# Two transformer layers on one core: one engine per PSUM tile, ScalarE takes the first plain copy of a slot, and the FFN norm is applied a slot later

## The chip, the cores and the metric

The kernel runs on one core of one Trainium2 chip. The metric is device time in microseconds; lower is better. TensorE (PE) does the matmuls, VectorE (DVE), ScalarE (ACT) and GpSimd (POOL) the element-wise work, and SyncE (SP) issues the DMAs. Each engine works through its own queue in order.

## The reference

Two blocks, run twice over x of 2048 rows and 512 columns in bfloat16. The attention block has 32 heads of 16 columns and a sliding window of 256 rows; the feed-forward block (FFN) is 512 to 1792 to 512 with ReLU.

```python
def _A_ref(x, wqkv, wo):
    ...
    scores = jnp.einsum("bhqd,bhkd->bhqk", q, k) * (Dh ** -0.5)
    ...
    mask = (idx[:, None] - idx[None, :] >= 0) & (idx[:, None] - idx[None, :] < W)
    scores = jnp.where(mask[None, None], scores, -1e9)
    p = _softmax(scores, axis=-1)
    o = jnp.einsum("bhqk,bhkd->bhqd", p, v)
    return (lambda x, *d: x.transpose(*d))(o, 0, 2, 1, 3).reshape(B, S, D) @ wo
...
x = x + _A_ref(_layernorm(x, axis=-1), A_wqkv, A_wo)
x = x + _B_ref(_layernorm(x, axis=-1), B_w1, B_w2)
x = x + _A_ref(_layernorm(x, axis=-1), A_wqkv, A_wo)
x = x + _B_ref(_layernorm(x, axis=-1), B_w1, B_w2)
```

## The kernel before

**Chunks and slots.** The rows are cut into four chunks of 512, so two layers make eight chunks, numbered 0 to 7 here. The program is a list of 160 slots (`NS`), 20 for each chunk (`SPS`). Slot s of chunk k does one group of attention scores for one of four head sets t and one of five groups of key blocks g: TensorE writes scores to the PSUM tile `Sps` (one buffer of four banks), ScalarE takes the exponential of it into `Pb`, and one slot later the group's triangular masks are laid on `Pb`, by GpSimd for g = 1 and 2 and by VectorE for the others. Five slots later, in slots with g of 1 to 4, TensorE multiplies `Pb` with V (24 matmuls into a tile `acc`), and VectorE divides by the sum into `O` (`pv_group`). So a slot with g = 0, which is slot 0, 5, 10 and 15 of a chunk, has no such product.

**The rest of the work fills the slots.** Projections to Q, K and V of the next chunk, the output projection `wo`, and the FFN (`w1`, then `w2`) are tasks cut into single matmuls. `run_tasks` takes tasks by earliest due slot, some nine matmuls a slot, two thirds of them ahead of the product with V and the rest behind it. A task can't start before its `early` slot. Each task accumulates in a PSUM tile `ps_d`, of which there are four, shared with `acc`, and is then copied out:

- Q (`q_items`): one copy of 128x512 to `Qt`, by ScalarE.
- K (`k_items`): two copies of the same tile to `KBD`, each with every second head set to zero by the factor `par`: the first by VectorE, the second by ScalarE (in chunks 1 and 6 each is split in two, since the ring of 20 key blocks wraps).
- V (`v_items`): four copies of 64x256 to `V2f`, by VectorE and ScalarE in turn.
- `w1` (`w1_item`): ReLU to `hT`, by VectorE. `wo` and `w2`: an addition to `x_sb`, by VectorE.

**From attention to the FFN.** In slots 1 to 4 of a chunk the last product with V of the chunk before comes out for rows j = 0 to 3; SyncE then transposes that `O` by DMA to `OT`, and `wo` for j may run two slots later. When `wo` for j = 1 and j = 3 is issued, `wo_done` calls `ln_rows`: VectorE takes the statistics of two row blocks, GpSimd finishes them (`rstdB`, `nbB`) and writes the normalised rows `xnB`, and SyncE transposes these to `xn2T`. All at once: `ln_rows` issues both the statistics and the application. With j = 3 the FFN tasks are planned, with their `early` slot three further on:

```python
def wo_done(k, j):
    ...
    if j % 2:
        ln_rows(c, xn2T[k], "B", j - 1, j + 1)
    if j == 3:
        plan_ffn(k, now[0] + 3)
```

**What sets the order.** `InOrder` chains TensorE, VectorE, ScalarE and GpSimd in the order of the code. SyncE is not chained: the framework's scheduler puts its DMAs in the order in which it expects them to become ready. The framework also puts a wait between two engines that read the same PSUM tile, so that they take it in turn.

Of the kernel before, what the change touches and what calls it, by code (L numbers as in the profile page):

```python
# [13 lines left out]
ACT = mybir.ActivationFunctionType  # L14
ALU = mybir.AluOpType
# [34 lines left out]
def kernel(  # L50
# [31 lines left out]
    chained = [True]  # L82
# [19 lines left out]
    pe, dve, act, pool = InOrder(nc.tensor), InOrder(nc.vector), InOrder(nc.scalar), InOrder(nc.gpsimd)  # L102
# [96 lines left out]
    def ln_rows(c, xnT, sfx, j0, j1):  # L199
        ln_apply(c, xnT, sfx, j0, j1, ln_stats(c, sfx, j0, j1))  # L200
# [2 lines left out]
    def slot(layer, kb):  # L203
        return (32 * layer + kb) % NSLOT

    def q_items(xnT, Qt, t, direct=False):
        ps = []

        def one(kc):
            if kc == 0:  # L210
                ps.append(ps_d.tile([P, 512], FP32, name="ps_d"))
            mm(ps[0][:], wqkv[:, kc, t * P:(t + 1) * P], xnT[:, kc, :], kc == 0, kc == KC - 1)
            if kc == KC - 1:
                (act.copy if chained[0] and not direct else dve.tensor_copy)(Qt[:], ps[0][:])
        return [lambda kc=kc: one(kc) for kc in range(KC)]

    def k_items(layer, c, xnT, t):
        ps = []
        s0 = slot(layer, 8 * c)
        runs = [(0, 8)] if s0 + 8 <= NSLOT else [(0, NSLOT - s0), (NSLOT - s0, 8)]  # L220

        def one(kc):
            if kc == 0:
                ps.append(ps_d.tile([P, 512], FP32, name="ps_d"))
            mm(ps[0][:], wqkv[:, kc, D + t * P:D + (t + 1) * P], xnT[:, kc, :], kc == 0, kc == KC - 1)
            if kc < KC - 1:
                return
            for a, b in runs:
                sa = (s0 + a) % NSLOT
                for e in range(2):  # L230
                    o = KBD[:, t, sa:sa + b - a, e, :]
                    i = ps[0][:, 64 * a:64 * b].rearrange("p (s k) -> p s k", k=64)
                    if e:
                        act.activation(o, i, ACT.Copy, scale=par[:, 1:2])
                    else:
                        dve.tensor_scalar(out=o, in0=i, scalar1=par[:, 0:1], scalar2=None, op0=ALU.mult)
        return [lambda kc=kc: one(kc) for kc in range(KC)]

    def v_items(layer, c, xnT, j):
        ps = []  # L240

        def one(kc):
            if kc == 0:
                ps.append(ps_d.tile([P, 512], FP32, name="ps_d"))
            mm(ps[0][:], xnT[:, kc, j * P:(j + 1) * P], wqkv[:, kc, 2 * D:3 * D], kc == 0, kc == KC - 1)
            if kc < KC - 1:
                return
            v4 = ps[0][:].rearrange("p (a e d) -> p e a d", e=2, d=16)
            for half in range(2):
                sl = slot(layer, 8 * c + 2 * j + half)  # L250
                for e in range(2):
                    (act.copy if e else dve.tensor_copy)(V2[64 * e:64 * e + 64, sl, e, :, 0:16],
                                                         v4[64 * half:64 * half + 64, e])
        return [lambda kc=kc: one(kc) for kc in range(KC)]


# [93 lines left out]
    def w1_item(xnT, hT, f):  # L350
        ps = []

        def one(kc):
            if kc == 0:
                ps.append(ps_d.tile([P, 512], FP32, name="ps_d"))
            mm(ps[0][:], w1[:, kc, f * P:(f + 1) * P], xnT[:, kc, :], kc == 0, kc == KC - 1)
            if kc == KC - 1:
                dve.tensor_relu(hT[:, f, :], ps[0][:])
        return [lambda kc=kc: one(kc) for kc in range(KC)]

    def w2_items(c, hT, j, final):
# [20 lines left out]
    NS = NSTEP * SPS  # L382
# [3 lines left out]
    def at_slot(s, fn):  # L386
        events.setdefault(s, []).append(fn)
# [53 lines left out]
    def plan_qkv(k, base):  # L441

        layer, c = divmod(k, NCH)

        def q_make(t):
            Q[k, t] = work.tile([P, 512], BF16, name="Qt", bufs=7)
            return q_items(xnTs[k], Q[k, t], t, k == 0)
        order = [("K0", 1), ("Q0", 2), ("K1", 3), ("Q1", 4), ("K2", 5), ("Q2", 6), ("K3", 7), ("V0", 8), ("V1", 9), ("V2", 10),
                 ("V3", 11), ("Q3", 12)]
        if k == 0:  # L450
            order = [("K0", 0), ("Q0", 0), ("V0", 1), ("V1", 1), ("V2", 1), ("V3", 1), ("K1", 2), ("Q1", 2), ("K2", 5),
                     ("Q2", 5), ("K3", 8), ("Q3", 8)]
        for what, due in order:
            n = int(what[1])
            if what[0] == "K":
                Task(base, base + due, base + SPS + 5 * n - 3, KC, lambda n=n: k_items(layer, c, xnTs[k], n))
            elif what[0] == "Q":
                Task(base + (6 if n == 3 else 1) if k else 0, base + due, base + SPS + 5 * n - 1, KC, lambda n=n: q_make(n))
            else:
                Task(base + 7 if k else 0, base + due, base + SPS + 3, KC, lambda n=n: v_items(layer, c, xnTs[k], n))  # L460
# [22 lines left out]
    def wo_done(k, j):  # L483
        layer, c = divmod(k, NCH)
        if j == 0:
            xn2T[k] = work.tile([P, KC, 512], BF16, name="xn2T", bufs=1)
        if j % 2:
            ln_rows(c, xn2T[k], "B", j - 1, j + 1)
        if j == 3:
            plan_ffn(k, now[0] + 3)  # L490

    now = [0]
    planned = [0]
# [30 lines left out]
    for s in range(NS + 5):  # L524
        now[0] = s
        u, g = divmod(s, 5)
        k, t = divmod(u, 4)
        layer, c = divmod(k, NCH)
        rest = sum(y.n for y in tasks) + 128 * (NSTEP - 1) - planned[0]
        budget = -(-rest // (NS - s)) if s < NS else 0  # L530
        has_pv = u >= 1 and g >= 1
        if s < NS:
            force(s)
            masks.append(attn_group(layer, c, t, g, Q[k, t], u % 2))
        for fn in events.pop(s, []):
            fn()
        done = run_tasks(s, -(-(budget + (3 if has_pv else 0)) // 2))
        if len(masks) > (1 if s < NS else 0):
            masks.pop(0)()
        if has_pv:  # L540
            pk, ptt = divmod(u - 1, 4)
            j = g - 1
            if ptt == 0 and j == 0:
                O_of[pk] = work.tile([P, 4, D], BF16, name="O", tag="O", bufs=1)
                chk_of[pk] = work.tile([P, 4, 32], FP32, name="chk")
            pv_group(pk // NCH, pk % NCH, ptt, j, (u - 1) % 2, O_of[pk], chk_of[pk])
            if ptt == 3:
                OTs[pk, j] = transpose_o(O_of[pk][:, j, :])
                plan_wo(pk, j, s + 2)
                if j == 3:  # L550
                    accumulate_check(chk_of[pk], badacc, first=(pk == 0))
        run_tasks(s, budget - done)
# [129 lines left out]
```

## Time and profile before

| What | us |
|---|---|
| median of two runs (619.52 and 620.05) | 619.78 |
| profiled execution | 618.08 |
| its span, first to last instruction | 616.4 |
| mean granted TensorE clock (share of full speed) | 0.905 |

The rows quoted below come from the profiled execution. Its own time is 1.7 us over its span, and 1.7 us under the median of the two other runs.

### The profile page before, as it was taken

What the parts mean: (1) busy time and instruction counts of PE and PEld (TensorE: products, weight loads), DVE (VectorE), ACT (ScalarE), POOL (GpSimd) and SP (SyncE); (2) the same over time, 40 slices, a digit from 0 to 9 for tenths busy, and PEclk for the clock granted to TensorE, in tenths of its full rate; (3) what the DMA queues carried; (4) which work ended last, traced back from release to release, by engine and by line L of the source; (5) the groups of instructions that cost most, each with busy time, mean ns of one, the idle gap of its engine ahead of it and who ended that gap; (6) DMA issues with size and microseconds to landing.
All of it is one profiled execution on the core that took longest, in us unless ns stands there. A gap on an engine that the chain in (4) does not pass through costs nothing.

```text
span 616.4 us, 13901 instructions
## 1 busy us (share of the span) xinstructions
PE 492.1 (80%) x5741; PEld 237.4 (39%) x5741; DVE 348.9 (57%) x919; ACT 345.9 (56%) x299; POOL 255.0 (41%) x558
## 2 busy tenths in 40 slices
PE   6748467689968998699958996799777996898395
PEld 2314233345423453344523442444433543344142
DVE  6444545477456847476456745685465637554461
ACT  2447668466757667566645565657737767462000
POOL 6562354437314544428224642446325444431300
PEclk9879659799978999899979998999988999898799
DMA  8610011201011011201110111002220013002201
GB/s 278 234 35 1 1 36 27 44 2 37 18 35 19 6 32 37 35 2 37 27 27 18 28 27 36 18 2 55 33 35 18 3 36 55 16 10 54 43 1 40
DMA packets 59001, 23.02 MB, mean 37 GB/s; under 512 B 50480, under 2 KB 58416, under 8 KB 58928
## 3 DMA queue, kind: packets, MB, share of 16 engines
q1 hardware_dynamic: 58928, 22.03, 15.6%
q8 instruction: 47, 0.77, 0.6%
q14 instruction: 26, 0.21, 0.1%
HBM read 7.86 MB, written 2.10 MB: 16 GB/s over the span
## 4 chain that ended last, share of the span: by engine, by line
PE 53%; ACT 16%; DVE 14%; DMA 5%; POOL 5%; issue 3%; SPq 2%; POOLq 0%; ACTq 0%; DVEq 0%
PE ps_d L94 40%; ACT Pb L94 12%; PE acc L94 7%; PE Sps L94 6%; DMA OT<-O 4%; DVE V2f L94 3%; ACT V2f L94 3%; DVE stB L94 2%; SPq L196 2%; POOL xnB L94 2%; DVE x_sb L94 2%; DVE KBD L94 2%; POOL rstdB L94 1%; DVE O L94 1%; DMA xnT<-xnA 1%
## 5 line engine op out<-in xcount | busy, mean ns | idle before, releaser
L94 ACT ACTIVATE Pb<-Sps 128x2048 bf16<-128x2048 f32 (+2 forms) x160 | 283.2, 1770 | 106.0 <-PE Sps L94 100.5
L94 POOL TENSOR_SCALAR_AFFINE_SELECT Pb<-Pb 64x256 bf16<-64x256 bf16 x368 | 154.2, 419 | 171.5 <-ACT Pb L94 146.5
L94 PE MATMUL ps_d<-xn2T,w 128*128 128x512 bf16 x448 | 118.9, 400 | 14.7 <-DMA xn2T<-xnB 13.2
L94 PE MATMUL ps_d<-w,hT 128*128 128x512 bf16 x448 | 110.8, 381 | 0.0
L94 PEld LDWEIGHTS <-Pb 128*128 128x128 bf16 x2880 | 92.6, 97 | 34.9 <-issue 9.1
L94 PE MATMUL Sps<-Qt,KBD 32*128 32x320 bf16 (+4 forms) x1408 | 64.6, 266 | 48.2 <-ACT Pb L94 46.8
L94 DVE TENSOR_SCALAR hT<-ps_d 128x512 bf16<-128x512 f32 x112 | 76.6, 687 | 38.5 <-PE ps_d L94 37.3
L94 PE MATMUL acc<-V2f,Pb 128*128 128x34 bf16 x2880 | 94.5, 180 | 0.9 <-DVE chk L94 0.8
L94 PE MATMUL ps_d<-xnT,wqkv 128*128 128x512 bf16 x256 | 78.1, 423 | 8.3 <-DMA xnT<-xnA 6.7
L94 PE MATMUL ps_d<-wo,OT 128*128 128x512 bf16 x128 | 40.3, 443 | 39.1 <-DMA OT<-O 39.1
L94 PEld LDWEIGHTS <-KBD 32*128 32x128 bf16 x1408 | 26.8, 93 | 115.2 <-issue 112.6
L94 PEld LDWEIGHTS <-w 128*128 128x128 bf16 x448 | 38.7, 100 | 61.7 <-issue 30.8
L94 DVE TENSOR_TENSOR x_sb<-ps_d,x_sb 128x512 f32<-128x512 f32 x48 | 32.9, 688 | 51.5 <-PE ps_d L94 50.9
L94 DVE TENSOR_TENSOR Pb<-Pb,tri 128x512 bf16<-128x512 bf16 (+1 forms) x152 | 59.9, 428 | 0.8 <-ACT Pb L94 0.8
L94 DVE RECIPROCAL chk<-acc 128x8 f32<-128x8 f32 x128 | 26.1, 204 | 59.4 <-PE acc L94 58.0
L94 POOL TENSOR_TENSOR rstdB<-rstdB,mhalf 128x2 f32<-128x2 f32 x16 | 12.0, 753 | 106.9 <-DVE rstdB L94 106.9
L94 PEld LDWEIGHTS <-hT 128*128 128x128 bf16 x448 | 37.9, 97 | 42.9 <-issue 6.6
L94 DVE CAST V2f<-ps_d 64x256 bf16<-64x256 f32 x64 | 27.0, 421 | 35.7 <-ACT V2f L94 32.9
L94 ACT ACTIVATE KBD<-ps_d,par 128x512 bf16<-128x512 f32 (+1 forms) x40 | 24.1, 604 | 38.2 <-DVE KBD L94 37.9
L94 DVE TENSOR_SCALAR KBD<-ps_d,par 128x512 bf16<-128x512 f32 (+1 forms) x40 | 25.5, 639 | 31.6 <-PE ps_d L94 21.1
L94 DVE TENSOR_TENSOR O<-acc,chk 128x128 bf16<-128x128 f32 x128 | 37.3, 291 | 8.9 <-DMA OT<-O 4.5
L94 ACT CAST V2f<-ps_d 64x256 bf16<-64x256 f32 x64 | 23.5, 368 | 31.2 <-DVE V2f L94 30.7
(65 smaller groups left out, 297.5 us busy)
## 6 DMA issues: line engine op xcount, KB each, us to landing
w<-in_B_w_dram SPq DMA_DIRECT2D x2, 1792.0 KB, 13.6
out_dram<-ob SPq DMA_DIRECT2D x16, 128.0 KB, 1.7
wqkv<-in_A_wqkv_dram SPq DMA_DIRECT2D x3, 512.0 KB, 6.7
xst<-in_A_x_dram SPq DMA_DIRECT2D x3, 512.0 KB, 8.7
xst<-in_A_x_dram SPq DMA_DIRECT2D x2, 256.0 KB, 2.9
wo<-in_A_wo_dram SPq DMA_DIRECT2D x1, 512.0 KB, 8.7
OT<-O SPq DMA_TRANSPOSE x32, 2.4
xn2T<-xnB SPq DMA_TRANSPOSE x32, 2.4
```

What stands on the lines that cost most here:

```text
L94: inst = fn(*a, **k)
L196: nc.sync.dma_start_transpose(out=xnT[:, :, j * P:(j + 1) * P], in_=xn[:].rearrange("p (kc d) -> p kc d", kc=KC))
```

## The change

There are three edits.

1. A new helper `evacuate` copies a PSUM tile out with one engine. In each slot after the first, the first plain copy (Q) or ReLU (`w1`) that the first call of `run_tasks` issues goes to ScalarE; all others go to VectorE.
2. The two copies of K and the four copies of V are all VectorE's.
3. `wo_done` takes the statistics as before but puts the application (`xnB` and its transposes) into a later slot: two slots on for j = 1 and one slot on for j = 3. The FFN may start four slots on, not three. After the last slot nothing is put off.

```diff
--- before.py
+++ after.py
@@ -203,7 +203,19 @@
     def slot(layer, kb):
         return (32 * layer + kb) % NSLOT
 
-    def q_items(xnT, Qt, t, direct=False):
+    act_turn = [False]
+
+    def evacuate(o, i, relu=False):
+
+        if act_turn[0]:
+            act_turn[0] = False
+            act.activation(o, i, ACT.Relu if relu else ACT.Copy)
+        elif relu:
+            dve.tensor_relu(o, i)
+        else:
+            dve.tensor_copy(o, i)
+
+    def q_items(xnT, Qt, t):
         ps = []
 
         def one(kc):
@@ -211,7 +223,7 @@
                 ps.append(ps_d.tile([P, 512], FP32, name="ps_d"))
             mm(ps[0][:], wqkv[:, kc, t * P:(t + 1) * P], xnT[:, kc, :], kc == 0, kc == KC - 1)
             if kc == KC - 1:
-                (act.copy if chained[0] and not direct else dve.tensor_copy)(Qt[:], ps[0][:])
+                evacuate(Qt[:], ps[0][:])
         return [lambda kc=kc: one(kc) for kc in range(KC)]
 
     def k_items(layer, c, xnT, t):
@@ -230,10 +242,7 @@
                 for e in range(2):
                     o = KBD[:, t, sa:sa + b - a, e, :]
                     i = ps[0][:, 64 * a:64 * b].rearrange("p (s k) -> p s k", k=64)
-                    if e:
-                        act.activation(o, i, ACT.Copy, scale=par[:, 1:2])
-                    else:
-                        dve.tensor_scalar(out=o, in0=i, scalar1=par[:, 0:1], scalar2=None, op0=ALU.mult)
+                    dve.tensor_scalar(out=o, in0=i, scalar1=par[:, e:e + 1], scalar2=None, op0=ALU.mult)
         return [lambda kc=kc: one(kc) for kc in range(KC)]
 
     def v_items(layer, c, xnT, j):
@@ -249,8 +258,7 @@
             for half in range(2):
                 sl = slot(layer, 8 * c + 2 * j + half)
                 for e in range(2):
-                    (act.copy if e else dve.tensor_copy)(V2[64 * e:64 * e + 64, sl, e, :, 0:16],
-                                                         v4[64 * half:64 * half + 64, e])
+                    dve.tensor_copy(V2[64 * e:64 * e + 64, sl, e, :, 0:16], v4[64 * half:64 * half + 64, e])
         return [lambda kc=kc: one(kc) for kc in range(KC)]
 
 
@@ -355,7 +363,7 @@
                 ps.append(ps_d.tile([P, 512], FP32, name="ps_d"))
             mm(ps[0][:], w1[:, kc, f * P:(f + 1) * P], xnT[:, kc, :], kc == 0, kc == KC - 1)
             if kc == KC - 1:
-                dve.tensor_relu(hT[:, f, :], ps[0][:])
+                evacuate(hT[:, f, :], ps[0][:], relu=True)
         return [lambda kc=kc: one(kc) for kc in range(KC)]
 
     def w2_items(c, hT, j, final):
@@ -444,7 +452,7 @@
 
         def q_make(t):
             Q[k, t] = work.tile([P, 512], BF16, name="Qt", bufs=7)
-            return q_items(xnTs[k], Q[k, t], t, k == 0)
+            return q_items(xnTs[k], Q[k, t], t)
         order = [("K0", 1), ("Q0", 2), ("K1", 3), ("Q1", 4), ("K2", 5), ("Q2", 6), ("K3", 7), ("V0", 8), ("V1", 9), ("V2", 10),
                  ("V3", 11), ("Q3", 12)]
         if k == 0:
@@ -485,9 +493,13 @@
         if j == 0:
             xn2T[k] = work.tile([P, KC, 512], BF16, name="xn2T", bufs=1)
         if j % 2:
-            ln_rows(c, xn2T[k], "B", j - 1, j + 1)
+            st = ln_stats(c, "B", j - 1, j + 1)
+            if now[0] >= NS:
+                ln_apply(c, xn2T[k], "B", j - 1, j + 1, st)
+            else:
+                at_slot(now[0] + (2 if j == 1 else 1), lambda: ln_apply(c, xn2T[k], "B", j - 1, j + 1, st))
         if j == 3:
-            plan_ffn(k, now[0] + 3)
+            plan_ffn(k, now[0] + 4 if now[0] < NS else now[0])
 
     now = [0]
     planned = [0]
@@ -534,7 +546,9 @@
             masks.append(attn_group(layer, c, t, g, Q[k, t], u % 2))
         for fn in events.pop(s, []):
             fn()
+        act_turn[0] = 0 < s < NS
         done = run_tasks(s, -(-(budget + (3 if has_pv else 0)) // 2))
+        act_turn[0] = False
         if len(masks) > (1 if s < NS else 0):
             masks.pop(0)()
         if has_pv:
```

Since the FFN tasks become ready one slot later, `run_tasks` fills the slots in another order from chunk 1 on. Counted from the order of TensorE's instructions: slot 9 of chunk 1 loses its nine FFN matmuls, slot 10 of chunk 2 and slot 9 of chunk 7 run none, and slots 10 of chunks 4 and 6 run one each. The FFN of each chunk therefore ends later, and in chunks 2 to 6 its last `w2` matmuls stand ahead of the third or fourth `wo` group.

**TensorE, chunk 2, the start of the products of slot 6** (`Sps` are scores, `OT` with `wo` is the output projection of j = 3, `hT` with `w_87`, which is `w2`, is the FFN). Before:

```order
L94 MATMUL Sps<-Qt,KBD 128x192
L94 LDWEIGHTS KBD
L94 MATMUL Sps<-Qt,KBD 128x192
L94 LDWEIGHTS OT
L94 MATMUL ps_d<-wo,OT 128x512
```

Now:

```order
L94 MATMUL Sps<-Qt,KBD 128x192
L94 LDWEIGHTS KBD
L94 MATMUL Sps<-Qt,KBD 128x192
L94 LDWEIGHTS hT
L94 MATMUL ps_d<-w_87,hT 128x512
```

The `wo` groups of j = 2 and 3 have moved behind 13 FFN matmuls (nine in slot 5 and four here); the one of j = 3 now ends in slot 7.

**SyncE, chunk 3 and the transposes of x for the next one** (`OT<-O` are the four attention outputs, `xn2T<-xnB` the normalised rows for the FFN, `xnT<-xnA` those for Q, K and V). Before:

```order
L332 DMA_TRANSPOSE OT<-O 128x4x128 x3
L196 DMA_TRANSPOSE xn2T<-xnB 128x4x128 x2
L332 DMA_TRANSPOSE OT<-O 128x4x128
L196 DMA_TRANSPOSE xn2T<-xnB 128x4x128 x2
L196 DMA_TRANSPOSE xnT<-xnA 128x4x128 x4
```

Now, with the start of chunk 4 behind it:

```order
L340 DMA_TRANSPOSE OT<-O 128x4x128 x4
L196 DMA_TRANSPOSE xn2T<-xnB 128x4x128 x4
L196 DMA_TRANSPOSE xnT<-xnA 128x4x128 x4
L340 DMA_TRANSPOSE OT<-O 128x4x128 x3
L196 DMA_TRANSPOSE xn2T<-xnB 128x4x128
```

In chunks 3 and 5 the last `O` is no longer behind two transposes of `xnB`; in chunks 1, 2, 4 and 6 one of the two is still ahead of it. In chunk 7 none was ahead before either.

**VectorE, chunk 3, from the product with V of slot 6** (a RECIPROCAL and the O behind it close one product; `V2f` are copies of V, `stB` to `rstdB` the statistics). Before:

```order
L94 RECIPROCAL chk<-acc 128x8
L94 TENSOR_TENSOR O<-acc,chk 128x128
L94 CAST V2f<-ps_d 64x16x16 x2
L94 RECIPROCAL chk<-acc 128x8
L94 TENSOR_TENSOR O<-acc,chk 128x128
L94 CAST V2f<-ps_d 64x16x16 x4
L94 RECIPROCAL chk<-acc 128x8
L94 TENSOR_TENSOR O<-acc,chk 128x128
L94 CAST V2f<-ps_d 64x16x16 x2
L94 TENSOR_SCALAR hT<-ps_d 128x512
```

Now, from the second statistics of that chunk on:

```order
L94 TENSOR_SCALAR rstdB<-mvB 128x2
L94 RECIPROCAL chk<-acc 128x8
L94 TENSOR_TENSOR O<-acc,chk 128x128
L94 TENSOR_TENSOR x_sb<-ps_d,x_sb 128x512
L94 RECIPROCAL chk<-acc 128x8
L94 TENSOR_TENSOR O<-acc,chk 128x128
L94 CAST V2f<-ps_d 64x16x16 x12
L94 TENSOR_TENSOR Pb_133<-Pb_133,tri 128x4x2x64
L94 TENSOR_TENSOR Pb_133<-Pb_133,tri 128x4x128
L94 RECIPROCAL chk<-acc 128x8
L94 TENSOR_TENSOR O<-acc,chk 128x128
L94 CAST V2f<-ps_d 64x16x16 x4
```

VectorE makes 16 copies of V in a chunk where it made eight, twelve of them in a row, behind the statistics. Over the kernel ScalarE loses 64 copies of V, 40 of K and six of Q and gains 45 ReLU; VectorE the reverse.

## Rows read from the trace of the kernel before

**Rows 1.** Part 1 of the page: busy time, share and instructions by engine.

```profile
PE 492.1 (80%) x5741; PEld 237.4 (39%) x5741; DVE 348.9 (57%) x919; ACT 345.9 (56%) x299; POOL 255.0 (41%) x558
```

**Rows 2.** Windows: chunk 3, its slots 5, 6, 8, 10, 11, and 5 to 11.

```profile
core 0: us, PE busy (x) PEld busy (x) DVE busy (x) ACT busy (x) POOL busy (x), PEclk, DMA share, GB/s
227.05:294.99 67.94, 58.31 (x749) 29.01 (x748) 42.57 (x112) 44.72 (x37) 31.07 (x68) 0.97 0.14 25
...
241.72:247.25 5.53, 2.23 (x16) 0.82 (x16) 4.74 (x16) 2.47 (x4) 2.67 (x5) 1.00 0.13 27
247.25:254.14 6.89, 4.37 (x42) 1.97 (x43) 2.34 (x7) 2.35 (x4) 0.00 (x0) 0.75 0.18 36
259.05:263.96 4.91, 2.94 (x45) 1.65 (x45) 2.10 (x7) 3.35 (x5) 3.30 (x9) 1.00 0.29 27
266.39:268.85 2.46, 2.46 (x18) 0.97 (x17) 1.77 (x4) 1.88 (x1) 0.00 (x0) 1.00 0.00 0
268.85:271.85 3.00, 3.00 (x42) 1.52 (x41) 2.31 (x6) 1.88 (x2) 1.00 (x2) 1.00 0.03 5
241.72:271.85 30.13, 20.81 (x244) 10.01 (x245) 18.50 (x52) 17.15 (x19) 11.32 (x24) 0.94 0.14 23
```

**Rows 3.** Timeline, chunk 3: start, us, engine, operation, [idle before <-releaser].

```profile
243.08 0.29 DVE L94 TENSOR_TENSOR O<-acc,chk 128x128 bf16<-128x128 f32 x1
...
246.66 0.69 ACT L94 ACTIVATE KBD<-ps_d,par 128x512 bf16<-128x512 f32 x1 [3.06 <-DVE KBD L94]
...
247.31 1.19 SPq L332 DMA_TRANSPOSE OT<-O  x1
...
249.77 0.61 PE L94 MATMUL ps_d<-wo,OT 128*128 128x512 bf16 x1 [5.34 <-DMA OT<-O]
```

**Rows 4.** Chain that ended last, chunk 3: start us, us, what.

```profile
239.76 0.69 DVE x_sb L94
...
243.84 1.53 POOL xnB L94 x2
...
245.92 1.22 SPq L196
...
247.31 2.41 DMA OT<-O
...
258.20 0.44 DVE V2f L94
...
258.66 0.38 ACT V2f L94
...
259.05 1.88 ACT Pb L94
...
266.29 1.83 PE ps_d L94 x8
```

**Rows 5.** Waits, whole kernel: who waited for whom, us in total, times, longest.

```profile
PE Sps L94 <- ACT Pb L94: 46.8, 42, 3.3
...
PE ps_d L94 <- DMA OT<-O: 39.1, 14, 6.3
...
PE ps_d L94 <- DMA xn2T<-xnB: 13.2, 2, 9.4
```

**Rows 6.** Groups of instructions by form, whole kernel: xcount | busy us, mean ns | idle before.

```profile
L94 POOL TENSOR_SCALAR_AFFINE_SELECT Pb<-Pb 64x256 bf16<-64x256 bf16 x368 | 154.2, 419 | 171.5 <-ACT Pb L94 146.5 <-PE acc L94 7.8
...
L94 DVE TENSOR_SCALAR hT<-ps_d 128x512 bf16<-128x512 f32 x112 | 76.6, 687 | 38.5 <-PE ps_d L94 37.3
...
L94 DVE CAST V2f<-ps_d 64x256 bf16<-64x256 f32 x64 | 27.0, 421 | 35.7 <-ACT V2f L94 32.9 <-PE ps_d L94 2.2
...
L94 ACT CAST V2f<-ps_d 64x256 bf16<-64x256 f32 x64 | 23.5, 368 | 31.2 <-DVE V2f L94 30.7
...
L94 DVE BATCH_NORM_STATS2 stB<-x_sb 128x6 f32<-128x512 f32 x32 | 21.5, 672 | 0.0
...
L94 DVE TENSOR_SCALAR KBD<-ps_d,par 128x512 bf16<-128x512 f32 x24 | 17.9, 744 | 14.3 <-PE ps_d L94 14.3
...
L94 ACT CAST Qt<-ps_d 128x512 bf16<-128x512 f32 x28 | 16.3, 588 | 27.7 <-PE ps_d L94 27.1
```

## The prediction

> **What bounds the kernel now.** I read the busy shares first: TensorE 80%, VectorE 57%, ScalarE 56% [rows 1]. Nothing is full, so the question is in which slots TensorE stands still. I therefore cut one regular chunk into its slots, from one exponential to the next [rows 2]. An undisturbed slot takes 2.46 us without a product with V (slot 10) and 3.00 us with one (slot 11); TensorE is busy all through both. Sixteen and four of these would make 57.8 us a chunk; chunk 3 takes 67.94. The ten microseconds lie in slots 5 to 8: 5.53 and 6.89, then twice 4.91 (slot 7 is as long as slot 8). Two mechanisms make them.
>
> *The wait for the last attention output.* TensorE stands 5.34 us ahead of the `wo` group of j = 3 [rows 3]. `O` is ready at 243.4, but its transpose is issued at 247.31: SyncE has two transposes of `xnB` ahead of it, and these wait on statistics, then GpSimd. The chain of waits runs through exactly this [rows 4]: x_sb at 239.76, `xnB` at 243.84, the second transpose at 245.92, `OT` at 247.31, landing 2.41 later. Over the kernel TensorE waits 39.1 us so [rows 5]; six long ones, one in each of chunks 1 to 6, make most of it. In that slot the clock falls to 0.75, and the four matmuls behind the wait pay for it.
>
> *The V copies.* VectorE and ScalarE take the same tile in turn, 0.44 and 0.38 us, with no overlap: 258.20, 258.66, then the exponential at 259.05 [rows 4]. The exponential of the next slot stands in ScalarE's queue behind four such hand-overs, and scores have one buffer, so TensorE waits for the exponential: 46.8 us over the kernel [rows 5].
>
> **The change part by part.** The sum is made against the span of 616.4 us; the median lies 3.4 us over it.
>
> *Slots 5 to 11 of a chunk, where the three edits meet.* They take 30.13 us with VectorE busy 18.50 [rows 2]. TensorE alone would need two slots of 2.46 and five of 3.00, 19.9 us: the floor if nothing waits. VectorE's own work in the new order, between the product of slot 4 and that of slot 11, is the other bound. To the 18.5 come eight V copies at 0.421, one K copy at 0.744, one Q copy and two additions (0.69 each, as the ReLU of the same shape), and a pair of statistics that has moved in (twice 0.672 and some 0.5 for the small steps); five ReLU copies of 0.687 go to ScalarE or later slots [rows 6]. That is 18.5 + 3.4 + 0.7 + 2.1 + 1.8 - 3.4 = 23.1 us. So the stretch ends between 19.9 + some stalls and 23.1. Lateness of VectorE can run on into slots 12 to 15, where the ReLU copies have become fewer, but twelve V copies in a row (5.1 us) must hold up the four tiles for a while. I take 22.7, a gain of 7.4, near VectorE's bound, since that is the row with the least freedom.
>
> That needs the wait for `OT` to be gone. In chunk 3 the transpose goes first in SyncE's new order: `O` at 243.4, issued at once, landing 2.4 later; TensorE reaches the group only after some 15 matmuls at 0.23 (eight take 1.83 [rows 4]) and two sets of scores, above 4 us. Covered. In chunks 2, 4 and 6 one transpose of `xnB` is still ahead. From the x_sb addition (239.76) to the first transpose's end is 6.1 us (245.9), and 2.5 more to landing: 8.6. TensorE has between 7 and 8.5 us of work before the group, thanks to the 13 or 14 `w2` matmuls. So waits of about 1.4, 0.6 and 0 remain, +2 in all. Five chunks (2 to 6): -37.
>
> *Chunk 1.* TensorE's order is the old one up to slot 8, so its wait stays and shortens by one transpose of 1.22 [rows 4]. The V slots gain: 9.8 + 2.4 + 2.5 before for slots 7 to 10, against some 12 of VectorE work. -4.
>
> *Chunks 0 and 7.* In chunk 0 the second K copy delays the first scores by 0.744, and two V slots can lose what slot 8 shows over slot 11, 1.9 each: between +0.7 and -3, taken -1. In chunk 7 TensorE waits 3.8 us for `xn2T` (13.2 less the 9.4 of the end [rows 5]); the FFN starts a slot later, so one product with V runs in that wait: between 0 and -2.5, taken -1. The tail behind the last slot is unchanged: there VectorE copies as before and the norm is not put off.
>
> *K copies in slots 1 to 4.* ScalarE's waits for VectorE delay an exponential there too, but TensorE has other matmuls: costed at nothing, the cover being its projections. VectorE's second copy, 0.744, lies in slots where it is idle a third of the time.
>
> *The ReLU and Q copies on ScalarE.* 1.88 for the exponential and 0.588 for a copy make 2.47 [rows 2, 6], within a slot of 3.00 and just that of 2.46. Waiting behind it is the next exponential; the copy's matmuls stand ahead of that exponential's scores on TensorE anyway. Nothing.
>
> *Slots without FFN work.* The later start leaves slots in which TensorE has no task. I price each slot at the larger of 2.46 and 0.53 + 0.213 a matmul + 0.52 for a product with V (this fits slots 10 and 11), over the counts of both orders, with the shorter exponentials of chunks 0 and 4: 432.8 us before, 438.7 now. +6.
>
> *The later norm.* In chunks 2 and 6 six mask steps of 0.419 (2.5 us) come ahead of `xnB` for j = 2, 3 on GpSimd. From the addition to landing the chain needs 9.9 us (239.76 to 247.2, and 2.4 [rows 4]); with the masks 12.4, against four slots, 11.4. A new wait of 1 us in two chunks: +2.
>
> Sum: -37 + 2 - 4 - 1 - 1 + 6 + 2 = -33 us. 619.8 - 33 = **587 us**.
>
> One rule speaks against the move of V to VectorE. The rows have a V copy at 0.421 us there and at 0.368 on ScalarE: 64 copies cost 3.4 us more, which is in the sum. The Trainium skill, Perfetto Trace Analysis, Optimizing Scalar/DVE Operations, gives VectorE the larger overhead on PSUM (~125 ns against ~51 ns) and would take work off VectorE where it is saturated. By its figures the 64 copies would cost an estimated 4.7 us more, so the sum would move by 1 us; its second half is the first rival.
>
> **The rivals.**
>
> 1. *VectorE is the bound and never catches up.* For: 23.1 of 30 us, then statistics of the next norm soon after. Against: from slot 11 on it is busy 2.31 of 3.00 [rows 2] and loses ReLU copies. Half the gain in five chunks is lost: -33 + 18 = -15, 605 us. Chance 0.2.
> 2. *Slower than before: the FFN waits for `xn2T` in each of seven chunks.* Such waits are there already, 3.8 and 9.4 us. If the fourth `wo` addition comes late, behind V copies (5.1 us), the chain of 9.9 to 12.4 becomes 15 to 17.5 against 11.4 us. It decides when VectorE is more than about 1.5 us behind at that addition. Some 5 us and 1 us of lower clock in seven chunks: +42, 629 us. Against: the order has the statistics ahead of the V copies. Chance 0.05.
> 3. *The edits meet no bound.* The wait for `OT` only turns into one for tiles, as the V copies still take 16 times 0.421 in series: 610 to 620 us. Against: the exponentials leave that series, 1.88 us each. Chance 0.07.
> 4. *All cover holds.* Slots 5 to 11 at 21 us: five times 1.7 more, no new waits: 574 us. Chance 0.1.
>
> **How the numbers follow.** The forecast, 576 to 600, has 0.58. The range reaches from rival 4 to rival 1 and a little beyond, 571 to 609. A measurement of this kernel tells about 2% from no change, that is below 607.4 or above 632. Faster by that: 0.58, 0.1, most of rival 1 and a little of rival 3, together 0.84. Same 0.12. Slower 0.04.
>
> **What would show it.** In the profile after: slots 5 and 6 at some 3 us with no wait for `OT` above 2 us in chunks 2 to 6, and one of about 4 in chunk 1; no ScalarE time in V or K; ScalarE's busy time down by some 25 us (V 23.5, K about 25 as on VectorE, six Q copies 3.5, against 45 ReLU at about 0.588 [rows 6]) and VectorE's up by as much; V slots at 3 to 4 us with VectorE full; slots without tasks at 2.46. The forecast is wrong if TensorE's wait for `xn2T` grows beyond some 6 us in all ahead of the tail, or if VectorE is full from slot 4 to slot 15.

## The result, and the profile after

The changed kernel takes 570.09 us (median of two runs, 569.97 and 570.20) against 619.78: a ratio of 0.9198, 95% interval 0.9159 to 0.9238. The forecast of 587 us had the direction and the two main mechanisms. But the gain is 49.7 us where it had 33, and the time lies 1 us under the low end of its range (571 to 609): on the size the prediction was wrong. The profiled execution has a span of 568.3 us (616.4 before).

Part 1 of the page, to be read against [rows 1]. VectorE's busy time has risen by 23.0 us and ScalarE's has fallen by 23.8; TensorE's share has risen to 83%.

```profile
PE 473.9 (83%) x5649; PEld 233.2 (41%) x5741; DVE 371.9 (65%) x984; ACT 322.1 (57%) x234; POOL 255.9 (45%) x558
```

Windows of chunk 3: the chunk, its slots 5, 6, 8, 10 and 11, and 5 to 11, as in [rows 2].

```profile
core 0: us, PE busy (x) PEld busy (x) DVE busy (x) ACT busy (x) POOL busy (x), PEclk, DMA share, GB/s
208.82:269.08 60.26, 56.81 (x741) 28.33 (x752) 45.94 (x119) 42.04 (x29) 31.77 (x68) 1.00 0.14 28
223.15:225.61 2.46, 2.33 (x17) 0.92 (x17) 2.36 (x9) 1.88 (x1) 0.00 (x0) 1.00 0.33 57
225.61:229.36 3.75, 3.36 (x41) 1.43 (x41) 3.68 (x9) 1.88 (x1) 2.55 (x5) 1.00 0.00 0
...
232.31:235.30 2.99, 2.88 (x45) 1.55 (x45) 2.39 (x10) 1.88 (x2) 2.11 (x5) 1.00 0.03 5
238.23:241.53 3.30, 2.59 (x17) 0.84 (x17) 3.16 (x8) 2.48 (x3) 2.90 (x7) 1.00 0.01 2
241.53:246.00 4.47, 3.45 (x41) 1.53 (x42) 4.33 (x12) 2.36 (x2) 2.32 (x5) 1.00 0.00 0
223.15:246.00 22.85, 20.38 (x244) 9.40 (x247) 21.60 (x58) 14.22 (x9) 12.84 (x27) 1.00 0.16 30
```

Slots 5 and 6 have come down from 5.53 and 6.89 us to 2.46 and 3.75, slot 8 from 4.91 to 2.99. The granted clock of slot 6 is 1.00, where it was 0.75. The stretch takes 22.85 us with VectorE busy 21.60. What it has over the 19.9 us of TensorE's own slots lies in slots 6, 10 and 11: TensorE waits there 0.29 and 1.09 us for VectorE (slots 6 and 11) and 0.57 us for the FFN's rows (slot 10). VectorE is the fullest engine of the stretch, but that it alone sets its length is not shown.

The timeline at the place of [rows 3]: `O`, its transpose, and the `wo` group that reads it.

```profile
222.84 0.29 DVE L94 TENSOR_TENSOR O<-acc,chk 128x128 bf16<-128x128 f32 x1
...
223.22 1.77 SPq L340 DMA_TRANSPOSE OT<-O  x1
...
226.14 0.82 PE L94 MATMUL ps_d<-wo,OT 128*128 128x512 bf16 x3
```

The transpose is issued 0.09 us after `O` is ready, where it was 3.9, and TensorE starts the group 2.9 us after the issue, with no idle time ahead of these matmuls.

The chain that ended last, in the same chunk, in place of [rows 4]:

```profile
230.34 0.60 DVE x_sb L94
230.94 0.61 DVE stB L94
...
232.92 0.72 POOL rstdB L94
...
234.31 1.53 POOL xnB L94 x2
235.84 0.46 SPq L196
236.39 2.43 DMA xn2T<-xnB
...
239.07 1.99 PE ps_d L94 x8
```

It no longer goes through `OT`, nor through copies in turn by two engines, but from the last addition of `wo` over the norm to `xn2T`: the FFN starts 0.25 us after its rows have landed, behind the 0.57 us of waiting for them. So the FFN, a slot later, has nothing to spare.

TensorE's waits over the kernel, against [rows 5]:

```profile
PE Sps L94 <- ACT Pb L94: 19.8, 20, 2.0
...
PE ps_d L94 <- DMA OT<-O: 14.7, 10, 4.9
PE ps_d L94 <- DMA xnT<-xnA: 11.9, 2, 11.0
PE ps_d L94 <- DMA xn2T<-xnB: 11.0, 3, 9.6
```

The two waits of the forecast have fallen from 46.8 and 39.1 to 19.8 and 14.7 us. Groups by form, against [rows 6]:

```profile
L94 DVE CAST V2f<-ps_d 64x256 bf16<-64x256 f32 x128 | 54.2, 423 | 3.3 <-PE ps_d L94 1.5
...
L94 DVE TENSOR_SCALAR KBD<-ps_d,par 128x512 bf16<-128x512 f32 x48 | 33.5, 743 | 14.9 <-PE ps_d L94 13.3 <-PE Sps L94 1.6
```

A copy of V or K costs VectorE what it did (0.421 and 0.744 us before); its idle time ahead of the V copies has gone from 35.7 us, 32.9 of it spent on ScalarE, to 3.3.

Where the time came from, from the starts of the exponentials in the two profiled executions (chunk k, slot s to slot t):

| Stretch | before | after | difference | forecast |
|---|---|---|---|---|
| chunk 0 | 64.84 | 58.87 | -6.0 | -1 |
| chunks 1 to 6, slots 0 to 4 (six summed) | 95.16 | 87.80 | -7.4 | 0 |
| chunk 1, slots 5 to 11 | 30.26 | 25.68 | -4.6 | -4 |
| chunks 2 to 6, slots 5 to 11 (five summed) | 150.89 | 118.59 | -32.3 | -33 |
| chunk 7, slots 5 to 11 | 24.52 | 22.13 | -2.4 | -1 |
| chunks 1 to 7, slots 12 on, and the tail | 214.91 | 219.41 | +4.5 | +6 |

The forecast of -33 for the five chunks is its -37 with the two terms of +2, for `OT` and for the later norm. Two rows vary between executions of the same code: chunk 0 takes 58.68 to 60.05 us in the eight profiled kernels that have the changed one's chunk 0, and the tail, from the start of the last exponential, 56.73 to 58.50 us over all 18 profiled kernels.

### The profile page after: what moved, and what is told of

Its sections match the earlier page's. It is cut to its first block, busy times and chain, and to the rows that moved or that the text cites. A ratio compares the mean times of both kernels' runs of the same rounds, so it can differ in the third digit from the quotient of the medians.

```text
span 568.3 us, 13813 instructions
## 1 busy us (share of the span) xinstructions
PE 473.9 (83%) x5649; PEld 233.2 (41%) x5741; DVE 371.9 (65%) x984; ACT 322.1 (57%) x234; POOL 255.9 (45%) x558
## 4 chain that ended last, share of the span: by engine, by line
PE 62%; DVE 19%; DMA 6%; POOL 5%; issue 4%; ACT 2%; SPq 0%; DVEq 0%; POOLq 0%; ACTq 0%
PE ps_d L94 46%; PE acc L94 9%; PE Sps L94 7%; DVE V2f L94 4%; DMA OT<-O 4%; DVE stB L94 3%; DVE x_sb L94 2%; DVE KBD L94 2%; DVE Pb L94 2%; ACT Pb L94 2%; DMA xn2T<-xnB 1%; DMA xnT<-xnA 1%; POOL xnA L94 1%; POOL xnB L94 1%; DVE O L94 1%
## 5 line engine op out<-in xcount | busy, mean ns | idle before, releaser
L94 PE MATMUL ps_d<-xn2T,w 128*128 128x512 bf16 x420 | 113.0, 399 | 16.9 <-DMA xn2T<-xnB 11.0
L94 PE MATMUL ps_d<-w,hT 128*128 128x512 bf16 x418 | 105.9, 379 | 4.5 <-issue 2.4
L94 PE MATMUL ps_d<-xnT,wqkv 128*128 128x512 bf16 x240 | 69.5, 405 | 17.0 <-DMA xnT<-xnA 11.9
L94 PE MATMUL Sps<-Qt,KBD 32*128 32x320 bf16 (+4 forms) x1408 | 64.2, 265 | 20.8 <-ACT Pb L94 19.8
L94 DVE TENSOR_SCALAR hT<-ps_d 128x512 bf16<-128x512 f32 x67 | 46.0, 687 | 30.4 <-PE ps_d L94 30.3
L94 DVE TENSOR_SCALAR KBD<-ps_d,par 128x512 bf16<-128x512 f32 (+1 forms) x80 | 46.7, 636 | 20.4 <-PE ps_d L94 18.0
L94 PEld LDWEIGHTS <-KBD 32*128 32x128 bf16 x1408 | 24.2, 93 | 84.3 <-issue 81.9
L94 DVE CAST V2f<-ps_d 64x256 bf16<-64x256 f32 x128 | 54.2, 423 | 3.3 <-PE ps_d L94 1.5
L94 PE MATMUL ps_d<-wo,OT 128*128 128x512 bf16 x119 | 35.7, 409 | 16.6 <-DMA OT<-O 14.7
L94 PEld LDWEIGHTS <-wqkv 128*128 128x128 bf16 x256 | 22.4, 101 | 43.3 <-issue 24.2
L94 PE MATMUL ps_d<-wqkv,xnT 128*128 128x512 bf16 x119 | 32.9, 396 | 0.9 <-issue 0.5
```

The lines of the kernel that those rows point to most:

```text
L94: inst = fn(*a, **k)
```

## The experiments

In short: **V** is the edit of the V copies, **K** that of K, **R** the helper for Q and ReLU, **N** the later norm with the later FFN. Chips differ by a few tenths of a per cent, so each run's ratio is to runs of the kernel before on its own chip; the changed kernel's is 0.9198.

**One edit alone.** V alone, from the kernel before:

```diff
-                    (act.copy if e else dve.tensor_copy)(V2[...], v4[...])
+                    dve.tensor_copy(V2[...], v4[...])
```

> The kernel before with the four copies of V on VectorE alone, nothing else changed. Theory (the exponential leaves the series of hand-overs, in every chunk): chunks 0 and 1 end as early as in the changed kernel, about 6 us each; chunks 2 to 6 lose the 1.9 us of two V slots but keep their wait for OT, about 4 each; together -30, 590 us. Rival (the FFN norm is what counts, V slots only fill time that the wait for OT leaves): under -12, above 608 us. Second rival (VectorE without the ReLU share is too full to take V): 615 to 625 us.

600.20 us, ratio 0.9674 (0.9604 to 0.9744): between the theory and its first rival. TensorE's two waits:

```profile
PE ps_d L94 <- DMA OT<-O: 39.4, 13, 6.3
PE Sps L94 <- ACT Pb L94: 22.1, 27, 3.6
```

The wait for the exponential halves, the one for `OT` stays. The two waits are separate, and V removes one of them. But chunk 0 fell only to 62.28 us, not to 59.

K alone:

```diff
-                    if e:
-                        act.activation(o, i, ACT.Copy, scale=par[:, 1:2])
-                    else:
-                        dve.tensor_scalar(out=o, in0=i, scalar1=par[:, 0:1], scalar2=None, op0=ALU.mult)
+                    dve.tensor_scalar(out=o, in0=i, scalar1=par[:, e:e + 1], scalar2=None, op0=ALU.mult)
```

> The kernel before with both copies of K on VectorE. Theory (slots 1 to 4 have other matmuls as cover, K matters little): -3 to +3, 617 to 623 us. Rival (the hand-over of K delays exponentials as that of V does; it is why slots 0 to 3 shortened by some 1.5 us a chunk): -10, 610 us.

610.64 us, ratio 0.9836 (0.9767 to 0.9905): clearly faster, though not clearly by 2%. The rival is right: slots 0 to 4 of chunks 1 to 6 lose 7.7 us together (95.16 to 87.45), chunk 6 alone 3.8.

R alone:

```diff
-                (act.copy if chained[0] and not direct else dve.tensor_copy)(Qt[:], ps[0][:])
+                evacuate(Qt[:], ps[0][:])
...
-                dve.tensor_relu(hT[:, f, :], ps[0][:])
+                evacuate(hT[:, f, :], ps[0][:], relu=True)
...
+        act_turn[0] = 0 < s < NS
```

> The kernel before with the first Q copy or ReLU of a slot on ScalarE and all other plain copies on VectorE; K and V still shared. Theory (VectorE isn't the bound while V is shared): -3 to +3 us. Rival (the offload is where a good part of the gain is from): -10 or more, below 610 us. Third: the ReLU joins ScalarE's queue ahead of exponentials that are late already: +5, 625 us.

617.93 us, ratio 0.9957 (0.9920 to 0.9995). The theory holds: 2.5 us or less.

N alone:

```diff
-            ln_rows(c, xn2T[k], "B", j - 1, j + 1)
+            st = ln_stats(c, "B", j - 1, j + 1)
+            ...
+                at_slot(now[0] + (2 if j == 1 else 1), lambda: ln_apply(...))
...
-            plan_ffn(k, now[0] + 3)
+            plan_ffn(k, now[0] + 4 if now[0] < NS else now[0])
```

> The kernel before with the FFN norm applied one or two slots after its statistics and the FFN planned one slot later; all copies as before. Theory (the wait for OT of 5 us in chunks 2 to 6 goes, five times some 4 us, and slots without FFN work cost less than the 6 us that the prediction put on them): -15 to -20, 600 to 605 us. Rival (with V still shared the time goes into waits for ScalarE instead): -5 to +5 us, 615 to 625.

605.74 us, ratio 0.9763 (0.9694 to 0.9832), just above the theory's band; faster, though not clearly by 2%. Both readings have a share in it:

```profile
PE Sps L94 <- ACT Pb L94: 61.6, 47, 4.1
...
PE ps_d L94 <- DMA OT<-O: 8.2, 6, 4.4
```

The wait for `OT` falls by 31 us, but 15 come back as waits for the exponential. Some five of these stand behind the V copies in turn. The other ten are three waits that the kernel before didn't have, of 4.0, 1.8 and 4.1 us in chunks 2, 4 and 6, each for an exponential behind a K copy that waits for VectorE's:

```profile
177.88 0.69 ACT L94 ACTIVATE KBD<-ps_d,par 128x512 bf16<-128x512 f32 x1 [4.49 <-DVE KBD L94]
...
180.39 0.61 PE L94 MATMUL Sps<-Qt,KBD 32*128 32x320 bf16 x8 [4.03 <-ACT Pb L94]
```

So what N frees is in good part taken by K's hand-over. Chunks 3 and 5 lose 6.7 and 7.7 us, chunks 1 and 2 gain 1.9 and 1.5.

**V and K without the rest** (both diffs above):

> The kernel before with K and V on VectorE alone, nothing else. Theory (in chunk 0 ScalarE's queue is held by V's and by K's turns one after the other, so only both together free it): chunk 0 near 59 us, as in the changed kernel, where V alone left 62.28 and K alone 64.72; in all 590 to 596 us. Rival (the ReLU share or another edit gives chunk 0 its gain): chunk 0 at 62 us or more.

594.91 us, ratio 0.9583 (0.9540 to 0.9626); chunk 0 takes 59.00 us, where V alone left 62.28 and K alone 64.71. So chunk 0's 6 us need both edits and no other.

**One edit undone in the changed kernel** (each diff above the other way round):

> The changed kernel with the four copies of V shared as before. Theory (V is worth 20 us alone, and some 20 to 25 in the whole): 590 to 596 us, slots 7 and 8 of most chunks above 4 us, chunk 0 above 63 us. Rival (the norm's edit already lets V slots go by): below 585 us.

595.28 us, ratio 0.9575 (0.9532 to 0.9617). Slots 7 and 8 of chunks 1, 2 and 4 last 4.27 to 5.86 us (2.60 to 4.48 in the changed kernel), chunk 0 64.27: the theory holds.

> The changed kernel with K's two copies shared between VectorE and ScalarE again. Theory (the K edit gave what the forecast put at nothing: slots 0 to 4 of chunks 1 and 6 above all): 576 to 580 us, slots 0 to 4 longer by some 8 us in all. Rival (with V and the ReLU share changed too, slots 0 to 4 have cover again): 568 to 573 us.

582.35 us, ratio 0.9419 (0.9381 to 0.9457): even more than the theory had. Slots 0 to 4 of chunks 1 to 6 take 96.52 us for 87.80, and chunk 0 is back at 62.17. The timeline of this kernel in chunk 0, slots 1 and 2:

```profile
24.59 1.24 ACT L94 ACTIVATE Pb<-Sps 128x1280 bf16<-128x1280 f32 x1 [1.06 <-PE Sps L94]
...
27.16 0.40 PE L94 MATMUL Sps<-Qt,KBD 32*128 32x192 bf16 x8
...
29.08 1.74 DVE L94 CAST V2f<-ps_d 64x256 bf16<-64x256 f32 x4
...
30.85 0.75 DVE L94 TENSOR_SCALAR KBD<-ps_d,par 128x512 bf16<-128x512 f32 x1
...
31.64 0.69 ACT L94 ACTIVATE KBD<-ps_d,par 128x512 bf16<-128x512 f32 x1 [5.81 <-DVE KBD L94]
32.22 1.87 ACT L94 ACTIVATE Pb<-Sps 128x2048 bf16<-128x2048 f32 x1
```

ScalarE stands still for 5.81 us. Its scores have been there since 27.6, but a K copy is ahead of the exponential in its queue, and that copy waits for VectorE's, which is behind the V copies. In the changed kernel the same exponential starts as soon as its scores are there:

```profile
26.95 0.40 PE L94 MATMUL Sps<-Qt,KBD 32*128 32x192 bf16 x8
...
27.40 1.88 ACT L94 ACTIVATE Pb<-Sps 128x2048 bf16<-128x2048 f32 x1 [1.79 <-PE Sps L94]
```

> The changed kernel with every Q copy on ScalarE and every ReLU on VectorE, as before; V, K and the norm as changed. Theory (the share is worth little, as alone, 2.5 us): 570 to 575 us. Rival (with V and K on VectorE too, VectorE is the bound in slots 5 to 11 and the share is what relieves it): 580 us or more, slots 5 to 11 of chunk 3 above 25 us with VectorE full.

569.25 us, ratio 0.9218 (0.9188 to 0.9248). The rival falls: slots 5 to 11 of chunk 3 take 22.39 us, and the share is worth nothing here. ScalarE then keeps six more Q copies, so VectorE is busy 21.34 us in that stretch, as good as before.

> The changed kernel with the FFN norm applied at once and the FFN planned three slots on, as before; all copies as changed. Theory (the edits add up: alone V was worth 20, K 10, the ReLU share 2.5, the norm 15): 586 to 590 us, with TensorE's wait for OT near 39 us. Rival (the copies alone run into the wait for OT, as K alone did in chunks 2 to 4): 593 to 600 us.

594.15 us, ratio 0.9605 (0.9576 to 0.9633): the rival. The wait for `OT` and its cause are as before:

```profile
PE ps_d L94 <- DMA OT<-O: 41.7, 14, 6.8
```

```profile
232.49 0.29 DVE L94 TENSOR_TENSOR O<-acc,chk 128x128 bf16<-128x128 f32 x1
...
234.04 2.50 SPq L196 DMA_TRANSPOSE xn2T<-xnB  x2
...
236.72 1.19 SPq L340 DMA_TRANSPOSE OT<-O  x1
...
239.17 0.61 PE L94 MATMUL ps_d<-wo,OT 128*128 128x512 bf16 x1 [5.82 <-DMA OT<-O]
```

Slots 5 and 6 of chunk 3 take 13.60 us together, where they took 12.42 in the kernel before: part of what the V and K copies no longer cost goes into this wait.

**What in N does it.** The norm at once, the FFN still a slot later:

```diff
-            if now[0] >= NS:
+            if True:
                 ln_apply(c, xn2T[k], "B", j - 1, j + 1, st)
```

> The changed kernel with the FFN norm applied at once but the FFN still planned four slots on. TensorE's order is that of the changed kernel. Theory (the FFN matmuls that now stand ahead of wo cover most of the wait for OT; the later application saves one transpose of 1.22 us in chunks 1, 2, 4 and 6): 570 to 576 us. Rival (the later application is what frees the queue of transposes): 580 us or more, with waits for OT above 4 us in chunks 2, 4 and 6.

573.21 us, ratio 0.9273 (0.9243 to 0.9303): the theory. Waits for `OT` of 3.2, 2.9 and 2.7 us are left in chunks 2, 4 and 6, where the changed kernel has 2.0, 1.7 and 2.0; chunks 3 and 5 have none. The other half, the norm later and the FFN as early as before:

```diff
-            plan_ffn(k, now[0] + 4 if now[0] < NS else now[0])
+            plan_ffn(k, now[0] + 3 if now[0] < NS else now[0])
```

> The changed kernel with the FFN planned three slots on as before, its norm still applied later. Theory (the FFN matmuls that stand ahead of wo are the cover, the later application only saves a transpose): 588 to 596 us, waits for OT near 35 us. Rival (the later application does it): 572 to 578 us.

587.88 us, ratio 0.9495 (0.9472 to 0.9519), 34.9 us of waits for `OT`. Of the 4.1% of the time before that N is worth in the changed kernel, the later FFN alone gives 3.3 and the later application alone 1.1. In chunks 2 and 4 SyncE's order is the old one in the first of these kernels, and yet they take 62.90 and 59.47 us against 66.68 and 63.45 with N undone: there TensorE has FFN matmuls to do while `OT` is on its way, and that alone is worth some 4 us a chunk. In chunks 3 and 5 the later FFN also puts all four `OT` first on SyncE, since all `wo` groups come behind FFN matmuls and the norm with them.

The application of j = 1 later still; nothing changes on TensorE and VectorE:

```diff
-                at_slot(now[0] + (2 if j == 1 else 1), ...)
+                at_slot(now[0] + (4 if j == 1 else 1), ...)
```

> The changed kernel with the norm of j = 1 applied four slots on, not two. TensorE's and VectorE's orders are those of the changed kernel; SyncE's has all four OT ahead of the transposes for xn2T in every chunk. Theory (what is left of the waits for OT is that one transpose and the norm ahead of it): no wait for OT above 2 us in chunks 1 to 6, -6 to -8 us, 562 to 564 us. Rival (the norm is then late for the FFN, since its four transposes of 1.22 us come in one piece): waits for xn2T of 2 us or more in most chunks, 572 to 585 us.

587.63 us, ratio 0.9496 (0.9466 to 0.9526): beyond the rival. Waits for `OT` are down to 7.3 us, but slot 10 of chunk 3 takes 9.42 us:

```profile
237.33 6.82 SPq L196 DMA_TRANSPOSE xn2T<-xnB  x4
...
245.62 3.57 PE L94 MATMUL ps_d<-xn2T,w 128*128 128x512 bf16 x8 [4.90 <-DVE V2f L94]
```

The profile puts the wait down to VectorE, but it is the FFN's rows: the last of the four transposes is issued at 242.93 and lands, by its semaphore, at 245.37. In each of chunks 1 to 7 TensorE waits ahead of its first FFN matmuls, 1.2 to 5.8 us. This is the waiting that the prediction's second rival describes.

**V on ScalarE**, in the changed kernel:

```diff
-                    dve.tensor_copy(V2[...], v4[...])
+                    act.copy(V2[...], v4[...])
```

> The changed kernel with all four copies of V on ScalarE, none on VectorE: one engine for a tile, but the one that makes the exponentials. Theory (the loss was that the exponential stands behind four steps of 0.44 and 0.38 us; now behind four of 0.37): the V slots last about 1.88 + 1.48 + 0.6 = 4 us where VectorE's copies allow 3, sixteen tiles in eight chunks of four at one each: 32 times some 0.5 to 1 us, 585 to 600 us. Rival (the turn-taking of two engines is all that matters; VectorE, 95% busy in slots 5 to 11, is relieved by four times 1.7 us a chunk): 565 to 573 us.

590.11 us, ratio 0.9530 (0.9507 to 0.9554): the theory. Slot 9 of chunk 3 lasts 4.83 us:

```profile
249.89 3.04 ACT L94 CAST V2f<-ps_d 64x256 bf16<-64x256 f32 x8
...
250.05 0.40 PE L94 MATMUL Sps<-Qt,KBD 32*128 32x256 bf16 x8
...
252.95 1.88 ACT L94 ACTIVATE Pb<-Sps 128x2048 bf16<-128x2048 f32 x1
```

The scores are there at 250.45, and the exponential starts 2.5 us later, behind eight copies. With no hand-over at all, slots 5 to 11 of chunks 2 to 6 take 130.2 us, hardly less than the 131.3 with V shared, against 118.6 with V on VectorE. So ending the turns gains little as long as the copies stay in ScalarE's queue: what costs is that the exponentials stand behind V's copies there, in turn or in a row. Whether the same holds for K, with both copies on ScalarE, no run shows.

**The FFN later still**: five slots on, then six.

```diff
-            plan_ffn(k, now[0] + 4 if now[0] < NS else now[0])
+            plan_ffn(k, now[0] + 5 if now[0] < NS else now[0])
```

> The changed kernel with the FFN planned five slots on, not four. SyncE's order then has all four OT first in chunks 2 to 6. Theory (FFN matmuls moved ahead of wo are the cover, so more of them take the rest of the waits for OT in chunks 2, 4 and 6, and the waits for xn2T shrink; slots without FFN work cost little): -6 to -10 us, 560 to 565 us. Rival (the price of empty slots, 6 us in the forecast, comes now, and the FFN of the last chunk ends later): 572 to 580 us.

558.04 us, ratio 0.9002 (0.8981 to 0.9023), better than the theory had. Slots 5 to 11 of chunk 3, and the waits:

```profile
222.14:243.28 21.14, 19.18 (x240) 9.33 (x243) 19.95 (x53) 14.12 (x9) 12.04 (x26) 1.00 0.16 32
```

```profile
PE ps_d L94 <- DMA xn2T<-xnB: 9.5, 2, 9.2
PE ps_d L94 <- DMA OT<-O: 9.3, 7, 4.9
```

Outside the tail 0.3 us of the wait for `xn2T` are left, and the one for `OT` of 4.9 is chunk 1's; chunks 2 to 6 have none that the trace shows. VectorE has less to do in the stretch (19.95 us for 21.60), since ReLU copies come later.

> The changed kernel with the FFN planned six slots on. Theory (five were enough to cover the waits; the sixth only adds slots without FFN work and a later end): +2 to +8 us over the 558 with five, 560 to 566 us. Rival (more cover helps on): below 557 us.

564.68 us, ratio 0.9087 (0.9048 to 0.9127): the theory. Of the 5.7 us of span that the sixth slot costs over the fifth, 3.0 are chunk 7 up to its last exponential (60.41 to 63.41), where FFN work has moved to; chunk 4 has 1.4 and the tail 1.2, which is within its spread. Waits for `OT` of 0.4 to 2.1 us are back in chunks 2 to 6.

Five slots, and in chunk 1 the norm of j = 1 three slots on:

```diff
-                at_slot(now[0] + (2 if j == 1 else 1), ...)
+                at_slot(now[0] + ((2 if k else 3) if j == 1 else 1), ...)
```

> The changed kernel with the FFN planned five slots on, and in chunk 1 the norm of j = 1 applied three slots on, so that SyncE has all four OT first there too. Theory (chunk 1 keeps its wait for OT of 4.9 us only for the norm's transpose ahead of it; without it, -1.2 to -2.5 us): 555.5 to 557 us. Rival (chunk 1 has no FFN matmuls to put ahead of wo, and the norm comes late for its FFN instead): 558 to 562 us.

554.63 us, ratio 0.8923 (0.8884 to 0.8962): the fastest, and a little under the theory's band. Chunk 1 goes from 66.42 to 64.74 us and the longest wait for `OT` from 4.9 to 3.0. So the transpose ahead of it was a part of that wait.

## Why the prediction was wrong, and what of it was right

The sum was 15 us short: -33 forecast, -48.1 measured in the span. The step that failed is the one on the K copies in slots 1 to 4, "costed at nothing, the cover being its projections": the runs showed 7.4 us there. The term for chunk 0, taken as -1, was mis-sized too, at -6.0 measured. The largest term and its two mechanisms were right.

**Right: slots 5 to 11 of chunks 2 to 6**, -33 forecast, -32.3 measured. Both mechanisms are shown: with N undone the wait for `OT` is back, with V undone that for the exponential. In chunk 3 the stretch takes 22.85 us where 22.7 were forecast, and VectorE, whose own 23.1 us were the reason, is busy 21.60 of it; that VectorE is the bound fits this but no run singles it out. Both reasons for which the wait for `OT` goes are the forecast's, SyncE's order in chunks 3 and 5 and the `w2` matmuls ahead of `wo` in 2, 4 and 6; the later FFN brings both, the later application little. In chunk 1, with the old order on TensorE, the wait stays at 4.9 us, where the forecast had about 4. That the sum came so near is in part luck: the waits for `OT` left in chunks 2, 4 and 6 are 5.7 us together where it had 2, chunk 5 has a wait of 2.7 for the FFN's rows that it didn't have, and against these the +2 for the later norm did not come and the stretch of chunk 4 is only 21.24 us long.

**Wrong: the K copies.** Slots 0 to 4 of chunks 1 to 6 lost 7.4 us in the changed kernel and 7.7 with K alone, and got 8.7 back with K undone. The prediction named the delay, an exponential behind a K copy that waits for VectorE's, and took TensorE's projections for its cover. ScalarE's idle time ahead of its K copies in the kernel before is no smaller than the 30.7 us ahead of its V copies [rows 6]:

```profile
L94 ACT ACTIVATE KBD<-ps_d,par 128x512 bf16<-128x512 f32 x24 | 16.5, 687 | 32.3 <-DVE KBD L94 32.0
```

In chunk 3, from which the prediction worked, the cover did hold: chunks 2 to 4 gained 0.3 us or less each. It failed in chunks 1, 5 and 6, where TensorE waited 2.3, 0.7 and 1.6 us for exponentials in these slots (0.5 in all afterwards) and which gained 1.7, 0.9 and 4.0. Chunks 1 and 6 are the two in which each K copy is split in two and a tile has four turns.

**Wrong in size: chunk 0, -1 forecast, -6.0 measured.** The forecast looked at the V slots, 8 and 9 (there 9.50 us became 5.43, -4.1, more than its best of -3) and took the second K copy of VectorE as a delay. In slots 0 and 1 the two queues were tied to each other by 16 V copies and the K copies behind them; the first two slots lost 3.9 us. So K's hand-over, put at nothing in slots 1 to 4, counts here too: with K undone chunk 0 takes 3.3 us more. Slot 4 gave 3.3 of it back: TensorE waits there for `xnT` and goes on at 44.83 us, where it was 44.99, so that transfer did not move.

**Slots without FFN work, +6 forecast, +4.5 measured**, and of that 3.3 are clear: slots 12 on of chunks 5, 6 and 7 got so much longer, with FFN matmuls that ran earlier before. The tail's 1.3 us lie within its spread. Slot 10 of chunk 2, with no matmul of a task, took 2.46 us as priced.

**The later norm, +2 forecast in chunks 2 and 6**, did not come. There is a wait of 2.68 us for the FFN's rows in chunk 5:

```profile
352.54 2.51 SPq L196 DMA_TRANSPOSE xn2T<-xnB  x2
...
358.61 0.91 PE L94 MATMUL ps_d<-xn2T,w 128*128 128x512 bf16 x2 [2.68 <-DVE Pb L94]
```

Slot 10 there took 6.93 us, which is contained in the -32.3 of the five chunks. But it isn't the later application's: with the norm applied at once TensorE waits 2.47 us at the same place. The second transpose lands late there in both kernels (the last section has more).

**ReLU and Q on ScalarE, nothing**: right, by both runs (alone and undone). Chunk 1 (-4, measured -4.6) and chunk 7's slots 5 to 11 (-1, measured -2.4) were near.

So of the 15 us, 7.4 are K in slots 0 to 4, 5.0 chunk 0, and the rest small terms. Either miss alone would have left the time within the range: with K worth nothing there it would be 577.5 us, with chunk 0 at -1 it would be 575.1. The rivals that lay above the forecast did not come; of the fourth, that all cover holds, the time came near, but not the reason: it had slots 5 to 11 at 21 us, where the five chunks have 23.7 on average; chunk 3 came to 21.1 only with the FFN five slots on.

On the rule that was weighed against V: the rows give 0.423 us for a V copy on VectorE and 0.367 on ScalarE, so moving all 128 there takes 54.2 us of work from the fuller engine and adds 47.0 to the other, and the kernel is 20 us slower. The Trainium skill, Perfetto Trace Analysis, Optimizing Scalar/DVE Operations, says that offloading some work to ScalarE may make sense if VectorE is saturated. In this kernel, with VectorE busy 21.60 of 22.85 us in the stretch, it did not pay: what stands behind the work in ScalarE's queue counts, not the engine's total. Why the two engines take turns at all, the Trainium skill tells in PSUM — Partial Sum Buffer, PSUM bank collisions raise a hardware error: two engines must be kept by semaphores from one bank and quadrant at a time. No run here shows what happens without.

## What to carry to other kernels

When two engines share the copies of one PSUM tile, whatever is queued behind on either engine can pay for each hand-over; look for the releaser "the other engine, same tile" in the idle column, for every tile that is shared and not for the longest alone, and in every stage and not in one regular chunk alone. Here it paid to give the whole tile to the engine whose queue TensorE waits for less, even if its single copy is slower and its total larger. The wait for a transfer was cheaper to cover here with matmuls that can be delayed (3.3% of the time) than to shorten by putting other transfers behind it (1.1%): plan the next stage later until its own input is no longer waited for, and stop where the displaced work shows at the end.

## What the runs showed that was not expected

- The edits neither add up nor overlap simply. Alone they gave 3.3, 1.6, 0.4 and 2.4% (V, K, R, N), which adds up to 7.7; all four gave 8.0. Undone from the whole, V costs 3.8 points of the time before, K 2.2, N 4.1 and R, within the intervals, nothing; that adds up to 10.1. The copies (V and K) on one side and N on the other each remove a wait that otherwise absorbs part of the other's gain.
- Of the two transposes for `xn2T` in chunk 5 quoted above, one took 2.4 us to landing and one 4.5; the second, issued at 353.82, landed at 358.37, and TensorE went on at 358.61. In its time falls one packet of 16 KB of a DMA queue of the kind "instruction". Over all 18 traces 241 of the 252 transposes that took more than 3 us to landing have a packet of 8 or 16 KB of such a queue starting between issue and landing, and only 203 of the 1404 others. That these packets cause the late landings is likely from this, but no run tests it.
- After a long wait TensorE can go on at a lower granted clock. In the kernel with the norm of j = 1 four slots on, eight FFN matmuls took 3.57 us behind 4.90 us of standing idle, at a granted clock of 0.50, its lower level (1.2 GHz):

```profile
245.62:249.19 3.57, 3.57 (x12) 1.09 (x16) 0.57 (x2) 0.60 (x1) 0.00 (x0) 0.50 0.00 0
```

  In the changed kernel the same eight took 1.99 us at 1.00 (2.4 GHz). So this wait cost 1.6 us more than its own length.
